# Attention and two gated feed-forward layers on one core: cosine argument rounded by a conversion to int32 on ScalarE, float64 words through a parametric ReLU

## Chip, cores, metric

One NeuronCore of one Trainium2 chip. The metric is the device time of one execution in microseconds (us), the median of several runs. Engines are called by the names of the profile: PE (TensorE), DVE (VectorE), ACT (ScalarE), POOL (GpSimd), SP (SyncE).

## What is computed

Four batches of 576 tokens, 8 heads of 64. Attention with a local mask (32 keys back) on half of the heads and a strided mask (every 32nd key) on the other half; its output, 2304 tokens by 512, runs through a layer with a cosine gate and then through a SiLU-gated layer. The weights arrive as float64.

```python
attn = softmax(mask(q @ k.T / sqrt(64)))          # per head
x = (attn @ v)                                     # 2304 x 512
h = x @ w_in                                       # 512 -> 2048
x = (h * np.cos(h)) @ w_out                        # 2048 -> 512
g, val = x @ w_gate, x @ w_val                     # 512 -> 1536 each
out = (g / (1 + np.exp(-g)) * val) @ w_out2        # 1536 -> 512
```

## The kernel before

**Stages.** One core does everything in three stages. The attention stage (until about 120 us of the span) goes through 48 groups of score tiles in a software pipeline, one step per group: matmuls for the scores (L365 to L368), maximum on DVE (L373), exponentials on ACT (L379), sums and reciprocals on DVE (L384, L388), normalisation on POOL (L389), transposes (L396, L400), copies out of PSUM on ACT (L407), the product with the values (L418) and its copy into xy (L431, L440). The first layer (until about 549 us) goes over 5 token blocks (four of 512, one of 256) and in each over 16 column tiles of w_in: such a pair is a slot. The second layer (to the end) does the same with 12 tiles of w_gate and w_val.

**Precision.** Each float32 matrix is split into a float16 high part (hi_part, L234, ACT) and a float16 low part (lo_part, L237, DVE), and every product is three float16 matmuls (mm3, L471 to L473). A slot has 12 matmuls of 512 columns for the up projection (up1), and 12 for the down projection (down1).

**Weights.** They are read as float64, 512 KB per tile of 128 by 512, as pairs of 32-bit words (load_raw, six raw buffers). conv_steps turns the words into float32: g0 multiplies the high word (read as a float32) by a power of two, on POOL in the attention stage and on ACT later; g1 takes the maximum (only for matrices that are scanned here); g2 shifts left by 3; g3 ORs in the top bits of the low word; g4 ORs in the sign of the high word and asks for the next tile. g1 to g4 are DVE instructions. w_in (16 tiles) is converted in the attention stage, w_out in the first slots of the first layer, w_gate and w_val after it, w_out2 at the end of the first layer and in the second.

**Cosine.** In slot s, up1_a turns the PSUM result ph into t = ph * turn + 1/4 (ACT, L503, into ta) and rounds t on POOL by adding and subtracting a large constant (L504), then subtracts t (L505, into tb). up1_b takes the sine on ACT (L508), one slot later; up1_c multiplies by ph on DVE (L512, which frees the PSUM bank), makes the high part on ACT (L513) and the low part on POOL (L514), two slots later. tb has three buffers, ta two, and the PSUM pool four banks.

**Order of the work.** All engines run in program order. Weight conversions lie in a list (fill) and are put between the slots by pump, which gets a budget in estimated DVE microseconds: PUMP per attention step, and in the first layer a share of the PE work of the slot. The down projections start after the first 23 up projections (HEAD = 21 plus the slots under way): until then a slot has only its 12 up matmuls and the converted g tiles are stored; after that one or two down projections come with each up projection until the stored ones are used up.

```python
later(0, hi_part ...); later(0.7, lo_part ...)      # split_chain, direct_later
budget = (work - 0.7 * n / 512) * SHARE             # work: estimated PE us of the slot
```

Of the kernel before, what the change touches and what calls it, by code (L numbers as in the profile page):

```python
# [10 lines left out]
F32 = mybir.dt.float32  # L11
F16 = mybir.dt.float16
BF16 = mybir.dt.bfloat16
I32 = mybir.dt.int32
AF = mybir.ActivationFunctionType
ALU = mybir.AluOpType
# [11 lines left out]
NBLK = len(BLOCKS)  # L28
# [11 lines left out]
MASKED = -1.0e9  # L40
MAGIC = 12582912.0
TWO_PI = 6.283185307179586
# [8 lines left out]
WARM = 11  # L51
PUMP, KP = 1.2, 5
XSAT = 9
EARLY, K0 = 1, 1
# [4 lines left out]
SHARE, SHARE2, SHARE3, SB = 0.95, 0.8, 0.4, 2  # L59
# [10 lines left out]
def build(tc, qk_l, qk_s, v_l, v_s, w_in, w_out, w_gate, w_val, w_out2, mask_l, mask_s, eye32, eye16, out):  # L70
    nc = tc.nc
    wide = w_in.dtype != F32
    with ExitStack() as ctx:
        keep = ctx.enter_context(tc.tile_pool(name="keep", bufs=1))
        ring = ctx.enter_context(tc.tile_pool(name="ring", bufs=2))
        small = ctx.enter_context(tc.tile_pool(name="small", bufs=1))
# [4 lines left out]
        quarter = small.tile([128, 1], F32, name="quarter")  # L81
        nc.vector.memset(quarter, 0.25)
        id16 = small.tile([128, 128], BF16, name="id16")
        ones16 = small.tile([128, 128], BF16, name="ones16")
# [77 lines left out]
        fill, emitted = deque(), set()  # L162
        beside_attention = True

# [21 lines left out]
        def conv_steps(mat, j, dst, scan):  # L186

            part = parts_w[mat][:, j:j + 1]
            box = {}
# [9 lines left out]
            def g0():  # L199

                t = raw[mat, j].popleft()
                box["h"], box["l"] = t[:, :, 1], t[:, :, 0]
                box["c"] = dst()
                box["u"] = box["c"].bitcast(I32)
                h = box["h"].bitcast(F32)
                if beside_attention:
                    nc.gpsimd.tensor_scalar(out=box["c"], in0=h, scalar1=2.0 ** -112, scalar2=1.0, op0=ALU.mult, op1=ALU.mult)
                else:
                    nc.scalar.activation(out=box["c"], in_=h, func=AF.Copy, scale=2.0 ** -112)

# [7 lines left out]
            def g3():  # L218
                u = box["u"]
                nc.vector.scalar_tensor_tensor(out=u, in0=box["l"], scalar=29, in1=u, op0=ALU.logical_shift_right, op1=ALU.bitwise_or)  # L220

            def g4():
                u = box["u"]
                nc.vector.scalar_tensor_tensor(out=u, in0=box["h"], scalar=-0x80000000, in1=u, op0=ALU.bitwise_and, op1=ALU.bitwise_or)  # L224
                load_raw()
            if not wide:
                return box, [(0.9 if scan else 0.35, f0)]
            return box, [(0, g0)] + [(0.63, g1)] * scan + [(0.36, g2), (0.63, g3), (0.63, g4)]

# [259 lines left out]
        acc_t, turn, c_y, half, c_o = {}, {}, {}, {}, {}  # L489
# [9 lines left out]
        def up1_a(c):  # L499
            n = c["n"]  # L500
            c["t"] = ring.tile([128, 512], F32, name="ta")[:, 0:n]
            c["w"] = ring.tile([128, 512], F32, name="tb", bufs=3)[:, 0:n]
            nc.scalar.activation(out=c["t"], in_=c["ph"], func=AF.Identity, scale=turn[c["blk"]], bias=quarter)  # L503
            nc.gpsimd.tensor_scalar(out=c["w"], in0=c["t"], scalar1=MAGIC, scalar2=MAGIC, op0=ALU.add, op1=ALU.subtract)  # L504
            nc.gpsimd.tensor_tensor(out=c["w"], in0=c["w"], in1=c["t"], op=ALU.subtract)  # L505

        def up1_b(c):
            nc.scalar.activation(out=c["w"], in_=c["w"], func=AF.Sin, scale=-TWO_PI)  # L508

# [135 lines left out]
        attn.close()  # L645
        beside_attention = False
        pacc = ctx.enter_context(tc.tile_pool(name="pacc", bufs=1, space=bass.MemoryType.PSUM))
# [80 lines left out]
        for blk in range(NBLK):  # L728
            for m in range(M1):
# [26 lines left out]
                up1_a(c)  # L756
                budget = (work - 0.7 * n / 512) * (SHARE3 if blk == NBLK - 1 else SHARE if blk < SB else SHARE2)
                pump_urgent()
# [100 lines left out]
```

## Time and profile before

| | us |
|---|---|
| median of 3 runs | 977.45 (975.25 to 980.06) |
| the profiled execution | 976.65 |
| its span, first to last instruction | 974.9 |
| busy in the span: PE, DVE, ACT, POOL | 912.2, 550.8, 393.4, 394.2 |
| mean granted clock of PE | 0.981 of full speed |

The span is cut into stretches below; in each, the engine to look at is the one whose wait ends last. Matmul durations in the trace overlap (a 512-column matmul is listed with 0.38 us and the next starts 0.215 us later), so the number of matmul records in a stretch tells how much PE work was done in it, and the busy time doesn't.

### The profile page before, as it was taken

The numbers are of one execution on the slowest core, as the hardware profiler recorded it, in microseconds if no ns is written. First come the engines' busy times: TensorE is split into PE (matmuls) and PEld (weight loads), VectorE is DVE, ScalarE is ACT, GpSimd is POOL, SyncE is SP. The second block draws the span as 40 slices with busy tenths as digits, with TensorE's granted clock in tenths as the row PEclk, the third lists the DMA queues.
The fourth block names the chain that finished last, engine by engine and source line by source line (L and its number), as shares of the span: only waits on it lengthen the run. The fifth ranks groups of instructions, "written<-read, shape, count | busy, mean of one in ns | idle before, by whom it ended". The sixth has DMA issues, their size and how long they took to land.

```text
span 974.9 us, 14438 instructions
## 1 busy us (share of the span) xinstructions
PE 912.2 (94%) x5608; PEld 473.8 (49%) x5608; DVE 550.8 (56%) x999; ACT 393.4 (40%) x829; POOL 394.2 (40%) x351
## 2 busy tenths in 40 slices
PE   7988986678799999899999999999999999999998
PEld 4666632233344444344458644444444444444587
DVE  5999776779992377895245387333323332332333
ACT  3776766554433234674346443222112221221122
POOL 3555389997557548699879400000000000000000
PEclk7999798999999999999999999999999999999999
DMA  9987741224430022207000020010001000100010
GB/s 307 348 272 200 227 167 57 65 65 126 135 108 22 22 86 88 66 1 259 1 23 22 22 65 1 1 44 1 1 1 44 0 1 1 44 1 1 1 45 22
DMA packets 21556, 72.14 MB, mean 74 GB/s; under 512 B 2704, under 2 KB 3472, under 8 KB 21488
## 3 DMA queue, kind: packets, MB, share of 16 engines
q1 hardware_dynamic: 21488, 71.22, 22.6%
q8 instruction: 44, 0.72, 0.3%
q14 instruction: 24, 0.20, 0.1%
HBM read 66.49 MB, written 4.72 MB: 73 GB/s over the span
## 4 chain that ended last, share of the span: by engine, by line
PE 66%; DVE 17%; POOL 10%; issue 4%; ACT 2%; DMA 1%; POOLq 0%; SPq 0%; ACTq 0%; DVEq 0%
PE bank L471 12%; PE bank L472 12%; PE bank L473 12%; PE acc L472 9%; PE acc L473 9%; PE acc L471 9%; POOL tb L504 5%; POOL tb L505 3%; POOL spare L514 2%; DVE spare L237 2%; DVE cv L224 1%; DVE wi L220 1%; DVE wi L224 1%; DVE ls L384 1%; DVE mx L373 1%
## 5 line engine op out<-in xcount | busy, mean ns | idle before, releaser
L471 PE MATMUL bank<-xs,spare 128*128 128x512 f16 (+1 forms) x480 | 171.7, 358 | 0.3 <-DVE ta L542 0.3
L473 PE MATMUL bank<-xs,spare 128*128 128x512 f16 (+1 forms) x480 | 171.7, 358 | 0.0
L472 PE MATMUL bank<-xs,spare 128*128 128x512 f16 (+1 forms) x480 | 171.7, 358 | 0.0
L504 POOL TENSOR_SCALAR tb<-ta 128x512 f32<-128x512 f32 (+1 forms) x80 | 148.5, 1857 | 51.1 <-ACT ta L503 45.3
L471 PE MATMUL bank<-xs,wi 128*128 128x512 f16 (+1 forms) x320 | 117.1, 366 | 38.1 <-DVE tb L512 29.5
L542 DVE SCALAR_TENSOR_TENSOR ta<-ta,bank 128x512 f32<-128x512 f32 (+1 forms) x60 | 38.0, 634 | 162.2 <-ACT ta L541 162.2
L472 PE MATMUL bank<-xs,wi 128*128 128x512 f16 (+1 forms) x320 | 117.3, 366 | 0.0
L473 PE MATMUL bank<-xs,wi 128*128 128x512 f16 (+1 forms) x320 | 117.0, 365 | 0.0
L541 ACT ACTIVATE ta<-bank,c 128x512 f32<-128x512 f32 (+1 forms) x60 | 38.6, 643 | 161.9 <-PE bank L473 161.9
L472 PEld LDWEIGHTS <-wi 128*128 128x128 f16 x560 | 55.2, 98 | 96.3 <-issue 46.1
L505 POOL TENSOR_TENSOR tb<-tb,ta 128x512 f32<-128x512 f32 (+1 forms) x80 | 97.1, 1213 | 6.7
L544 ACT ACTIVATE g<-ta 128x512 f16<-128x512 f32 (+1 forms) x60 | 35.3, 588 | 132.2 <-DVE ta L543 132.2
L472 PE MATMUL acc<-g,wi 128*128 128x512 f16 (+1 forms) x240 | 85.8, 358 | 0.2 <-DVE g L545 0.2
L471 PE MATMUL acc<-g,wi 128*128 128x512 f16 (+1 forms) x240 | 85.8, 358 | 0.0
L473 PE MATMUL acc<-g,wi 128*128 128x512 f16 (+1 forms) x240 | 85.8, 358 | 0.0
L471 PEld LDWEIGHTS <-wi 128*128 128x128 f16 x560 | 55.4, 99 | 62.2 <-issue 9.3
L473 PEld LDWEIGHTS <-wi 128*128 128x128 f16 x560 | 55.3, 99 | 56.5 <-issue 3.9
L503 ACT ACTIVATE ta<-bank,quarter,c 128x512 f32<-128x512 f32 (+1 forms) x80 | 58.0, 725 | 56.2 <-PE bank L473 52.6
L512 DVE SCALAR_TENSOR_TENSOR tb<-tb,bank 128x512 f32<-128x512 f32 (+1 forms) x80 | 50.3, 628 | 43.4 <-ACT tb L508 43.2
L472 PEld LDWEIGHTS <-spare 128*128 128x128 f16 x480 | 47.0, 98 | 46.7 <-issue 0.6
L471 PEld LDWEIGHTS <-spare 128*128 128x128 f16 x480 | 47.0, 98 | 46.4
L473 PEld LDWEIGHTS <-spare 128*128 128x128 f16 x480 | 47.0, 98 | 46.4
(127 smaller groups left out, 1602.6 us busy)
## 6 DMA issues: line engine op xcount, KB each, us to landing
raw<-w_out SPq DMA_DIRECT2D x56, 512.0 KB
raw<-w_in SPq DMA_DIRECT2D x16, 512.0 KB
raw<-w_gate SPq DMA_DIRECT2D x12, 512.0 KB
raw<-w_val SPq DMA_DIRECT2D x12, 512.0 KB
qks<-qk_s SPq DMA_DIRECT2D x8, 594.0 KB
qkl<-qk_l SPq DMA_DIRECT2D x8, 592.0 KB
out<-xy SPq DMA_DIRECT2D x16, 256.0 KB
vl<-v_l SPq DMA_DIRECT2D x8, 432.0 KB
```

Source lines behind the costliest of these rows:

```text
L224: nc.vector.scalar_tensor_tensor(out=u, in0=box["h"], scalar=-0x80000000, in1=u, op0=ALU.bitwise_and, op1=ALU.bitwise_or)
L237: nc.vector.scalar_tensor_tensor(out=dst, in0=src, scalar=s, in1=hi, op0=ALU.mult, op1=ALU.subtract)
L471: nc.tensor.matmul(out=o, lhsT=w[:, 0, c], rhs=x[0], start=first, stop=False)
L472: nc.tensor.matmul(out=o, lhsT=w[:, 0, c], rhs=x[1], start=False, stop=False)
L473: nc.tensor.matmul(out=o, lhsT=w[:, 1, c], rhs=x[0], start=False, stop=last)
L503: nc.scalar.activation(out=c["t"], in_=c["ph"], func=AF.Identity, scale=turn[c["blk"]], bias=quarter)
L504: nc.gpsimd.tensor_scalar(out=c["w"], in0=c["t"], scalar1=MAGIC, scalar2=MAGIC, op0=ALU.add, op1=ALU.subtract)
L505: nc.gpsimd.tensor_tensor(out=c["w"], in0=c["w"], in1=c["t"], op=ALU.subtract)
L512: nc.vector.scalar_tensor_tensor(out=w, in0=w, scalar=2.0 ** -14, in1=c["ph"], op0=ALU.mult, op1=ALU.mult)
L541: nc.scalar.activation(out=t, in_=pg, func=AF.Tanh, scale=half[blk])
L542: nc.vector.scalar_tensor_tensor(out=t, in0=t, scalar=1.0, in1=pg, op0=ALU.add, op1=ALU.mult)
L544: nc.scalar.activation(out=g[:, 0, 0:n], in_=t, func=AF.Copy)
```

## The change

The rounding leaves POOL. ACT now writes t = ph * turn + 1/4 as int32 into tb, by which it is rounded; up1_b forms ph * turn minus that integer on DVE (a new instruction, reading PSUM) and ACT takes sin(2 pi x + pi/2) with the bias in a one-column tile. L504 and L505 and the tile ta of the first layer are gone. In conv_steps the multiplication g0 is a parametric ReLU on ACT in all stages: with the slope 2^32 for negative inputs the exponent's bit that is moved into the sign's place by the shift is set, so g4 is gone. Budgets are reset: PUMP 1.2 to 1.0, XSAT 9 to 12 (where in the list the scale of the first token block stands), and 1.25 instead of 0.7 us of DVE taken off the budget of each slot.

```diff
-PUMP, KP = 1.2, 5
-XSAT = 9
+PUMP, KP = 1.0, 5
+XSAT = 12
...
+        right = small.tile([128, 1], F32, name="right")
+        nc.vector.memset(right, TWO_PI / 4)
...
-                if beside_attention:
-                    nc.gpsimd.tensor_scalar(out=box["c"], in0=h, scalar1=2.0 ** -112, scalar2=1.0, op0=ALU.mult, op1=ALU.mult)
-                else:
-                    nc.scalar.activation(out=box["c"], in_=h, func=AF.Copy, scale=2.0 ** -112)
+                nc.scalar.activation(out=box["c"], in_=h, func=AF.Prelu, scale=2.0 ** -112, alpha=2.0 ** 32)
...
-            def g4():
-                u = box["u"]
-                nc.vector.scalar_tensor_tensor(out=u, in0=box["h"], scalar=-0x80000000, in1=u, op0=ALU.bitwise_and, op1=ALU.bitwise_or)
                 load_raw()
...
-            return box, [(0, g0)] + [(0.63, g1)] * scan + [(0.36, g2), (0.63, g3), (0.63, g4)]
+            return box, [(0, g0)] + [(0.63, g1)] * scan + [(0.36, g2), (0.63, g3)]
...
-            c["t"] = ring.tile([128, 512], F32, name="ta")[:, 0:n]
             c["w"] = ring.tile([128, 512], F32, name="tb", bufs=3)[:, 0:n]
-            nc.scalar.activation(out=c["t"], in_=c["ph"], func=AF.Identity, scale=turn[c["blk"]], bias=quarter)
-            nc.gpsimd.tensor_scalar(out=c["w"], in0=c["t"], scalar1=MAGIC, scalar2=MAGIC, op0=ALU.add, op1=ALU.subtract)
-            nc.gpsimd.tensor_tensor(out=c["w"], in0=c["w"], in1=c["t"], op=ALU.subtract)
+            nc.scalar.activation(out=c["w"].bitcast(I32), in_=c["ph"], func=AF.Identity, scale=turn[c["blk"]], bias=quarter)
 
         def up1_b(c):
-            nc.scalar.activation(out=c["w"], in_=c["w"], func=AF.Sin, scale=-TWO_PI)
+            nc.vector.scalar_tensor_tensor(out=c["w"], in0=c["ph"], scalar=turn[c["blk"]], in1=c["w"].bitcast(I32),
+                                           op0=ALU.mult, op1=ALU.subtract)
+            nc.scalar.activation(out=c["w"], in_=c["w"], func=AF.Sin, scale=TWO_PI, bias=right)
...
-                budget = (work - 0.7 * n / 512) * (SHARE3 if blk == NBLK - 1 else SHARE if blk < SB else SHARE2)
+                budget = (work - 1.25 * n / 512) * (SHARE3 if blk == NBLK - 1 else SHARE if blk < SB else SHARE2)
```

In the changed file the lines stand at other numbers: the write as int32 is L496, the new DVE subtraction L499, the sine L501, the product with ph L505, high part L506, low part on POOL L507; g0 is L207, g1 L210, g2 L214, g3 L218, hi_part L228, lo_part L231, and L367, L378, L382 are the maximum, the sums and the reciprocals of the attention. The order of the instructions on three engines at the places that the prediction speaks of follows; names end in the number of the tile.

ACT in the head of the first layer (the slots before the first down projection), before, about one slot; a name in brackets is an engine that the instruction waits for:

```order
L508 ACTIVATE tb_2445<-tb_2445 128x512 [waits Activation_49,Pool_49]
L503 ACTIVATE ta_2504<-bank_2491,quarter_89,c6_2001 128x512 [waits PE_49,Activation_49]
L234 ACTIVATE xs_2449<-xy1_67,s10_2421 128x512
L234 ACTIVATE wo3_2143<-cv_2394,s8_2325 128x512 [waits DVE_49]
L209 ACTIVATE cv_2512<-raw_2230 128x512 [waits DMAHW1_49,Activation_49]
L513 ACTIVATE spare14_2172<-tb_2445 128x512 [waits DVE_49]
```

And in the changed kernel, two slots:

```order
L501 ACTIVATE tb_2499<-tb_2499,right_91 128x512 [waits DVE_49]
L496 ACTIVATE tb_2552<-bank_2539,quarter_89,c6_1992 128x512 [waits PE_49,Pool_49]
L506 ACTIVATE spare10_2148<-tb_2499 128x512 [waits DVE_49]
L501 ACTIVATE tb_2525<-tb_2525,right_91 128x512 [waits DVE_49]
L496 ACTIVATE tb_2578<-bank_2565,quarter_89,c12_2563 128x512 [waits DVE_49,PE_49,Pool_49]
L228 ACTIVATE wo4_2124<-cv_2506,s8_2346 128x512
L207 ACTIVATE cv_2581<-raw_2314 128x512 [waits DMAHW2_49]
L506 ACTIVATE spare9_2147<-tb_2525 128x512 [waits DVE_49]
```

The sine no longer waits for POOL but for DVE; the first instruction of a slot (L496) now waits for POOL, which must have read the tb buffer that it overwrites, the one of three slots before.

DVE at the same place, before, one slot and the start of the next:

```order
L512 SCALAR_TENSOR_TENSOR tb_2505<-tb_2505,bank_2491 128x512
L216 TENSOR_SCALAR cv_2512<-cv_2512 128x512
L237 SCALAR_TENSOR_TENSOR wo4_2144<-cv_2455,s8_2325,wo4_2144 128x512
L220 SCALAR_TENSOR_TENSOR cv_2512<-raw_2230,cv_2512 128x512
L224 SCALAR_TENSOR_TENSOR cv_2512<-raw_2230,cv_2512 128x512
L512 SCALAR_TENSOR_TENSOR tb_2534<-tb_2534,bank_2520 128x512
```

And in the changed kernel:

```order
L499 SCALAR_TENSOR_TENSOR tb_2552<-bank_2539,c6_1992,tb_2552 128x512
L218 SCALAR_TENSOR_TENSOR cv_2534<-raw_2234,cv_2534 128x512
L505 SCALAR_TENSOR_TENSOR tb_2552<-tb_2552,bank_2539 128x512
L214 TENSOR_SCALAR cv_2581<-cv_2581 128x512
L231 SCALAR_TENSOR_TENSOR wo5_2125<-cv_2534,s8_2346,wo5_2125 128x512
L499 SCALAR_TENSOR_TENSOR tb_2578<-bank_2565,c12_2563,tb_2578 128x512
```

Each slot has two instructions on the cosine instead of one, the sign's OR is gone, and fewer steps of the conversion stand in a slot.

DVE in the attention stage, before, one tile of w_in beside the steps of the attention:

```order
L212 TENSOR_REDUCE pw_in_94<-raw_497 128x1
L216 TENSOR_SCALAR wi10_81<-wi10_81 128x512
L220 SCALAR_TENSOR_TENSOR wi10_81<-raw_497,wi10_81 128x512
L388 RECIPROCAL ls_859<-ls_859 128x4
L384 TENSOR_REDUCE ls_900<-e_l1_121 128x3
L373 TENSOR_REDUCE mx_914<-bank_905 128x3
L224 SCALAR_TENSOR_TENSOR wi10_81<-raw_497,wi10_81 128x512
```

And in the changed kernel:

```order
L210 TENSOR_REDUCE pw_in_96<-raw_502 128x1
L382 RECIPROCAL ls_826<-ls_826 128x3
L378 TENSOR_REDUCE ls_861<-e_s1_119 128x4
L367 TENSOR_REDUCE mx_878<-bank_867 128x4
L214 TENSOR_SCALAR wi11_82<-wi11_82 128x512
L218 SCALAR_TENSOR_TENSOR wi11_82<-raw_502,wi11_82 128x512
```

A tile of w_in has three DVE steps instead of four; its multiplication is an ACT instruction now.

## Rows read from the trace of the kernel before

**Rows 1.** Busy time by stretch: us, engines (records), granted clock, DMA share, GB/s

```profile
20.00:92.00 72.00, 66.94 (x1088) 47.55 (x1088) 70.22 (x178) 52.35 (x210) 42.32 (x60) 0.98 0.89 285
92.00:109.00 17.00, 15.46 (x164) 10.66 (x162) 12.82 (x39) 11.73 (x40) 4.06 (x7) 0.60 0.71 214
127.00:210.00 83.00, 55.85 (x227) 23.18 (x226) 58.55 (x85) 49.07 (x80) 80.25 (x54) 0.94 0.24 78
210.00:270.00 60.00, 50.13 (x223) 22.15 (x223) 55.38 (x76) 28.30 (x47) 41.72 (x27) 0.97 0.38 114
270.00:400.00 130.00, 128.85 (x599) 58.42 (x598) 82.47 (x129) 48.58 (x81) 81.97 (x58) 1.00 0.21 67
400.00:510.00 110.00, 104.74 (x511) 49.73 (x510) 65.98 (x115) 58.11 (x100) 92.58 (x67) 1.00 0.20 70
510.00:556.00 46.00, 43.76 (x368) 35.67 (x367) 21.73 (x50) 22.77 (x52) 35.70 (x42) 1.00 0.08 24
```

**Rows 2.** POOL's groups, 127 to 210 us: busy us, mean ns, idle before

```profile
L504 POOL TENSOR_SCALAR tb<-ta 128x512 f32<-128x512 f32 x17 | 35.0, 2058 | 1.3
L505 POOL TENSOR_TENSOR tb<-tb,ta 128x512 f32<-128x512 f32 x18 | 23.9, 1328 | 1.5
L514 POOL TENSOR_TENSOR spare<-tb,spare 128x512 f16<-128x512 f32 x17 | 22.3, 1313 | 0.0
```

**Rows 3.** DVE timeline: the first L512 and the one 18 slots later

```profile
127.02 0.69 DVE L512 SCALAR_TENSOR_TENSOR tb<-tb,bank 128x512 f32<-128x512 f32 x1
...
209.84 0.69 DVE L512 SCALAR_TENSOR_TENSOR tb<-tb,bank 128x512 f32<-128x512 f32 x1 [1.24 <-ACT tb L508]
```

**Rows 4.** Waits, 127 to 210 us: total us, times, longest us

```profile
PE bank L471 <- DVE tb L512: 20.1, 10, 3.1
```

**Rows 5.** DVE's groups, 127 to 210 us

```profile
L220 DVE SCALAR_TENSOR_TENSOR cv<-raw,cv 128x512 int32<-128x512 int32 x10 | 13.8, 1381 | 0.0
L512 DVE SCALAR_TENSOR_TENSOR tb<-tb,bank 128x512 f32<-128x512 f32 x19 | 12.9, 681 | 14.7 <-ACT tb L508 14.6
L224 DVE SCALAR_TENSOR_TENSOR cv<-raw,cv 128x512 int32<-128x512 int32 x9 | 7.8, 869 | 0.1
L237 DVE SCALAR_TENSOR_TENSOR wo<-cv,s,wo 128x512 f16<-128x512 f32 x9 | 7.8, 864 | 8.9 <-ACT wo L234 8.9
```

**Rows 6.** DVE's groups, 20 to 112 us (the attention stage)

```profile
L224 DVE SCALAR_TENSOR_TENSOR wi<-raw,wi 128x512 int32<-128x512 int32 x16 | 13.2, 824 | 0.2
...
L237 DVE SCALAR_TENSOR_TENSOR wi<-wi,s,wi 128x512 f16<-128x512 f32 x6 | 4.5, 744 | 0.1
```

**Rows 7.** DVE timeline: one L220 while POOL was idle

```profile
251.69 0.69 DVE L220 SCALAR_TENSOR_TENSOR spare<-raw,spare 128x512 int32<-128x512 int32 x1
```

**Rows 8.** ACT's groups, 127 to 210 us

```profile
L503 ACT ACTIVATE ta<-bank,quarter,c 128x512 f32<-128x512 f32 x19 | 14.5, 761 | 0.0
L508 ACT ACTIVATE tb<-tb 128x512 f32<-128x512 f32 x18 | 11.3, 629 | 25.0 <-POOL tb L505 25.0
L513 ACT ACTIVATE spare<-tb 128x512 f16<-128x512 f32 x18 | 11.3, 628 | 8.1 <-DVE tb L512 7.6
...
L234 ACT ACTIVATE wo<-cv,s 128x512 f16<-128x512 f32 x9 | 6.4, 708 | 0.8 <-DVE cv L224 0.8
```

**Rows 9.** PE timeline: mask matmuls (one ends each attention step), and one stall

```profile
26.80 0.29 PE L368 MATMUL bank<-ml,id 128*128 128x288 bf16 x1
...
60.52 0.29 PE L368 MATMUL bank<-ml,id 128*128 128x288 bf16 x1
...
75.46 0.29 PE L368 MATMUL bank<-ml,id 128*128 128x288 bf16 x1
...
92.11 0.29 PE L368 MATMUL bank<-ml,id 128*128 128x288 bf16 x1
94.44 0.22 PE L123 MATMUL bank<-tops,ones 128*128 128x128 bf16 x1 [1.54 <-DVE tops L117]
```

**Rows 10.** Groups of the whole span: one of the three table loads

```profile
L508 ACT ACT_TABLE_LOAD x1 | 1.3, 1283 | 0.0
```

More of the change, by code (lines that the diff above doesn't have):

```diff
@@ L40 @@
 MASKED = -1.0e9
-MAGIC = 12582912.0
 TWO_PI = 6.283185307179586
@@ L162, in build @@
         fill, emitted = deque(), set()
-        beside_attention = True
         def later(cost, fn, key=None):
@@ L645, in build @@
         attn.close()
-        beside_attention = False
         pacc = ctx.enter_context(tc.tile_pool(name="pacc", bufs=1, space=bass.MemoryType.PSUM))
```

## The prediction

> **What bounds the kernel now.** I read the table of busy times by stretch first, because PE's own work is fixed: the change leaves every matmul in place and in its order, so time can only come out of stretches in which PE is not fed. PE work in a stretch is its matmul records times 0.215 us, the distance at which 512-column matmuls follow each other (128.85 us for 599 of them between 270 and 400) [rows 1]. From 127 to 210 us PE did 227 x 0.215 = 48.8 us of work in 83, so 34.2 us were lost; from 210 to 270, 223 x 0.215 = 47.9 of 60, 12.1 lost; from 400 to 510 it idled 5.3 and from 510 to 556 2.2 by its busy time [rows 1]. From 270 to 400, and in the second layer, there is nothing to win.
>
> What starves PE from 127 to 210 is POOL: it is busy 80.25 of 83 us [rows 1], and its three instructions of a slot take 2.06 + 1.33 + 1.31 = 4.70 us [rows 2]. The slots follow at exactly that pace: 18 of them between the two L512 shown, (209.84 - 127.02) / 18 = 4.60 us [rows 3], while a slot's 12 matmuls need 12 x 0.215 = 2.58. PE feels it as a wait for the bank that L512 frees [rows 4]. From 210 to 270 the picture is another: DVE is busy 55.38 of 60 us [rows 1]; there the conversion of w_out and w_gate sets the pace.
>
> **The head, 18 slots.** The change takes L504 and L505 off POOL, which keeps 1.31 us a slot [rows 2] and stops being the bound. What comes next? PE's floor is 2.58. For DVE I start from its 58.55 busy us [rows 1]. The nine L224 go: -7.8 [rows 5]. By the order of the instructions 18 slots of the changed kernel hold 3 ORs (L218) and 2 low parts fewer than 18 slots before, since the budget of a slot is smaller: -3 x 1.38 - 2 x 0.86 = -5.9 [rows 5]. Added are 18 subtractions L499. No row shows one; it is bounded by L512 (one PSUM, one SBUF operand, 0.681) [rows 5] and by L237 in the attention stage, which like it has a per-partition factor (0.744) [rows 6]; I take 0.744: +13.4. That makes 58.3, or 3.24 us a slot, if instructions stay as slow as they were beside a busy POOL. They don't all: L220 took 1.38 on average there and 0.69 in a moment with POOL idle [rows 5, 7], L237 0.864 against 0.744 [rows 5, 6], while L512, with one operand in PSUM, kept 0.68. Were all of it given back (7 x 0.69 + 12 x 0.12 = 6.2 us), DVE would need 52.1 us, 2.89 a slot. POOL's share falls from 97% to 1.31 / 3.05 = 43%, so I give back 57%: 54.8, 3.05 a slot. The Trainium skill ("SBUF — State Buffer", Who interferes with whom) says that a DVE instruction with two SBUF inputs and a POOL instruction that reads SBUF exclude each other for a whole instruction, and that one with a single SBUF input is not touched. The trace agrees (1.38 against 0.69 for L220, 0.68 for L512); by that rule L499, which reads PSUM, is never held up, and without it the sum would stay at 3.24.
>
> ACT: 49.07 us busy [rows 1]; the write as int32 replaces a write as float32 in the same instruction and I leave its 0.761 [rows 8]. The sine now has a bias column, which I price like L234 with its one factor column, 0.708 instead of 0.629 [rows 8]: +1.4. So 50.5 / 18 = 2.80 a slot. A new wait: L496 of a slot can't overwrite tb before POOL has read it for the low part of three slots before. That ring is high part 0.628, low part 1.31, next write 0.761 [rows 8, 2], 2.70 us, and 3.41 where one more conversion of 0.71 [rows 8] stands between write and high part on ACT, which the order shows in about a third of the slots. Queued behind a late L496 are the high part and the sine, and for these DVE waits. Four limits between 2.58 and 3.05 that hand over to each other in order: I take **3.05** and keep 2.6 and 3.4 as the ends. Gain: 18 x (4.60 - 3.05) = **27.9**; ends 34.2 (all that PE lost) and 18 x 1.2 = 21.6.
>
> **210 to 270.** DVE loses an L224 per tile and gains an L499 per slot; a slot here carries up to four tiles. At 0.869 [rows 5] against 0.744 [rows 6], some 19 ORs less and 10 subtractions more, minus the steps that the head left over (about 6, the 5.9 us above), it is near balance: -16.5 + 7.4 + 5.9 = -3.2 us, and on top of that POOL blocks less, since it is left with one instruction of 1.31 in slots of some 7 us (1 up and nearly 2 down projections, 34 x 0.215 = 7.3). PE's work then exceeds DVE's. Of the 12.1 lost I take **8** back; ends 3 and 12.
>
> **Attention.** DVE is busy 70.22 of 72 us [rows 1]; 16 L224 of 0.824 leave it, 13.2 us [rows 6]. From the mask matmul at 26.80 to that at 92.11 there are 32 steps, 2.04 us each; where PE is fed without a break (60.52 to 75.46, 8 steps) a step takes 1.87 [rows 9]. So at most 32 x 0.17 = 5.4 us are there. Against it stands that the 16 multiplications by POOL become ACT instructions; priced as the conversions that ACT already does, 0.71 [rows 8], they bring ACT from 52.35 of 72 us [rows 1] to about 63, close behind PE, and PE waits for ACT's copies in every step. I take **3**, ends 0 and 5.4. After 92 us PE stood 1.54 us for a scale from DVE [rows 9], and the granted clock between 92 and 109 was 0.60 [rows 1], mostly the lower level, 1.2 GHz. At the higher level the same 17 us would be 10.2; that 6.8 us goes into no forecast, because the changed order has the same scale in the same place.
>
> **Last slots of the first layer.** From 510 to 556 POOL's chain is shorter and PE's 2.2 us and part of the 5.3 before may close: **2**, ends 0 and 5. Nothing in the second layer: there the change only removes the sign's OR for a few tiles of w_out2, beside PE.
>
> **Sum.** 27.9 + 8 + 3 + 2 = 40.9 us off the profiled execution's 976.65: **936** (rounded). That execution is 0.8 us under the median of the runs, which the range takes in.
>
> **Rivals.**
> - *Deeper.* PE runs the head at its own pace (34), the second stretch closes but for 2 us (10), and DVE, no longer behind, has the scale ready, so that the clock doesn't fall at 92 us (6.8), with 5 in the attention steps and 3 at the end: 976.65 - 58.8 = about 918. For it: all engines' sums in the head are within 0.5 us of PE's. Against it: DVE at 3.05, and the same place of the scale.
> - *Shallower.* The tb ring and the bursts on DVE add up instead of overlapping and a head slot takes 3.6: 18.0, with 3 from the second stretch, 1 and 1 from the rest: 954. It decides once the ring's extra conversion (3.41) falls in most slots. For it: L496 waits for POOL in every slot of the order. Against: three buffers let two slots pass.
> - *ACT's write as int32 is slow.* Only at 0.761 + 1.80 = 2.56 us would ACT hold the slot at 4.60; the head then gains nothing, the rest about 5: 972, within half a percent. No row shows a write as int32 on ACT; its writes as float16 and float32 take the same 0.63 [rows 8].
> - *Slower.* The ring lets only one slot through at a time: write, subtraction, sine, product, high part, low part in series, 0.761 + 0.744 + 0.708 + 0.681 + 0.628 + 1.313 = 4.83 us. The head would lose 18 x 0.23 = 4, and of the later slots the some 30 that carry conversions would take 4.83 + 0.69 + 0.74 = 6.26 where PE has 24 x 0.215 = 5.16: 33 more, 976.65 + 37 - 3 = about 1011. It decides when a slot's chain and the conversions queued in it exceed 5.16. Against it: POOL, busy 1.31 a slot, would have to be late by two slots.
> - *Table loads.* If the parametric ReLU were in another table than exponential and sine, each of the 68 tiles would cost two loads of 1.28 us [rows 10], 174 us: 1110. The order of the changed kernel has three table loads, as many as before, so I give it 1 in 100. The Trainium skill ("ScalarE: Activation LUTs", What ACT_TABLE_LOAD costs) asks 2.66 us for every switch to another set; by that figure it would be an estimated 362 us instead of 174.
>
> **How the numbers follow.** Forecast 0.60, deeper 0.15, shallower 0.17, slow write 0.04, slower 0.03, table loads 0.01. The forecast's own range, from the ends of its terms, is about 925 to 948; down to 918 it takes in half of the deeper case, up to 954 half of the shallower one, which leaves some 2 in 10 outside. Half a percent (5 us) is about what a measurement of this kernel can tell from no change: faster 0.92, within it 0.04, slower 0.04.
>
> **What would show it.** POOL without L504 and L505 and idle for more than half of the head; 18 slots between products on DVE in about 55 us instead of 82.8; DVE the busiest engine there, at over 90%; L218 nearer 0.7 than 1.4; L499 at 0.70 to 0.75; L496 at 0.76; attention steps under 2.0 us; the second layer as long as before. I am wrong if the head's slots take over 3.4 us (then look whether L496 waits for POOL), if ACT's write or the parametric ReLU takes over 0.9 us, or if PE's clock falls in other places of the attention stage.

## The result, and the profile after

The changed kernel takes 949.6 us in the median of four runs (942.45 to 955.63); the kernel before, measured beside it, 977.6. The ratio is 0.971 [0.9633, 0.9787]. The forecast was 936, with a range from 918 to 954. The profiled execution of the changed kernel is one of the four: 946.87 us, span 944.9. By its marks the 30.0 us between the two spans (974.9 and 944.9) lie here:

| stretch | forecast | measured | marks before, after |
|---|---|---|---|
| until the first product with ph | 3 | 4.0 | 127.02, 123.00 |
| the head, 18 slots | 27.9 | 18.2 | 82.82, 64.62 |
| from there to the first store of block 0 | 8 | 8.9 | 75.41, 66.49 |
| the rest | 2 | -1.1 | 689.65, 690.79 |

The first product is the first L505 (L512 before), and the store of block 0 is its copy out of PSUM. One term is off by much, the head. The two products that bound it, in DVE's timeline of the changed kernel (start, us, instruction, idle time before and its releaser), answer to [rows 3]:

```profile
123.00 0.69 DVE L505 SCALAR_TENSOR_TENSOR tb<-tb,bank 128x512 f32<-128x512 f32 x1 [1.97 <-ACT tb L501]
...
187.62 0.69 DVE L505 SCALAR_TENSOR_TENSOR tb<-tb,bank 128x512 f32<-128x512 f32 x1 [0.89 <-ACT tb L501]
```

(187.62 - 123.00) / 18 = 3.59 us a slot, where 4.60 were before and 3.05 were forecast. Busy time by stretch in the changed kernel, with the columns of [rows 1]:

```profile
20.00:92.00 72.00, 71.41 (x1034) 50.77 (x1032) 57.83 (x168) 57.06 (x214) 26.70 (x44) 0.83 0.92 292
92.00:109.00 17.00, 17.00 (x281) 12.26 (x280) 15.87 (x44) 16.88 (x64) 6.62 (x11) 1.00 0.81 256
123.00:188.00 65.00, 51.64 (x226) 22.28 (x225) 51.80 (x88) 48.53 (x76) 21.03 (x20) 0.97 0.24 75
188.00:258.00 70.00, 67.27 (x311) 30.37 (x311) 58.20 (x104) 41.00 (x65) 13.10 (x11) 1.00 0.52 158
```

POOL, which was busy 97% of the head, is busy 32% of it now. But no other engine took its place as the bound: PE's busy time is 79% of the head, DVE's 80%, ACT's 75%. In a stage in which no engine is busy throughout, they wait for each other. The groups of that stretch (busy us, mean ns, idle before and its releasers) show that no instruction is much dearer than its price in the forecast:

```profile
L507 POOL TENSOR_TENSOR spare<-tb,spare 128x512 f16<-128x512 f32 x18 | 21.0, 1164 | 53.7 <-ACT spare L506 41.5 <-DMA raw<-w_out 12.1
L496 ACT ACTIVATE tb<-bank,quarter,c 128x512 int32<-128x512 f32 x19 | 14.6, 768 | 4.3 <-PE bank L124 2.4 <-POOL spare L507 1.9
L499 DVE SCALAR_TENSOR_TENSOR tb<-bank,c,tb 128x512 f32<-128x512 f32 x18 | 13.4, 743 | 0.0
L505 DVE SCALAR_TENSOR_TENSOR tb<-tb,bank 128x512 f32<-128x512 f32 x19 | 13.0, 685 | 5.4 <-ACT tb L501 5.2
L501 ACT ACTIVATE tb<-tb,right 128x512 f32<-128x512 f32 x18 | 12.9, 719 | 10.4 <-DVE tb L499 10.4
L231 DVE SCALAR_TENSOR_TENSOR wo<-cv,s,wo 128x512 f16<-128x512 f32 x6 | 6.5, 1075 | 4.9 <-ACT wo L228 4.9
L207 ACT ACTIVATE cv<-raw 128x512 f32<-128x512 f32 x9 | 5.8, 655 | 0.0
L218 DVE SCALAR_TENSOR_TENSOR cv<-raw,cv 128x512 int32<-128x512 int32 x7 | 5.6, 802 | 0.0
```

The subtraction takes 0.743 us (0.744 was priced), the write as int32 0.768 (0.761), the sine with a bias column 0.719 (0.708), the OR 0.802, between the 1.38 and the 0.69 of before [rows 5, 7]. The waits of the same stretch (total us, times, longest):

```profile
PE bank L465 <- DVE tb L505: 12.9, 7, 4.8
ACT tb L501 <- DVE tb L499: 10.4, 12, 1.8
DVE tb L505 <- ACT tb L501: 5.2, 12, 2.0
DVE wo L231 <- ACT wo L228: 4.9, 6, 1.6
DVE q L125 <- PE bank L124: 3.2, 1, 3.2
ACT tb L496 <- POOL spare L507: 1.9, 4, 0.7
DVE cv L214 <- ACT cv L207: 1.2, 1, 1.2
```

DVE waits 5.2 + 4.9 + 3.2 + 1.2 = 14.5 us in these rows; 1.97 of them stand ahead of the first product, which leaves 12.5 for the head. Its work, 51.80 us, makes 2.87 a slot. So DVE had less to do than the 3.05 of the forecast, and the other 0.7 us of a slot's 3.59 are waiting. They aren't spread evenly. The short slots (1 to 4, 14 and 17, counted from the first product on) take 2.73 to 2.89 us; slots 5 and 6 take 5.05 and 5.73, slot 9 4.71, slot 12 5.20, slots 15 and 16 4.01 and 4.57. The timeline of slot 12, the engines together in order of time:

```profile
162.65 0.78 ACT L496 ACTIVATE tb<-bank,quarter,c 128x512 int32<-128x512 f32 x1 [0.71 <-POOL spare L507]
163.32 0.62 ACT L506 ACTIVATE spare<-tb 128x512 f16<-128x512 f32 x1
...
163.84 0.71 ACT L228 ACTIVATE wo<-cv,s 128x512 f16<-128x512 f32 x1
...
164.02 1.16 POOL L507 TENSOR_TENSOR spare<-tb,spare 128x512 f16<-128x512 f32 x1 [1.41 <-ACT spare L506]
...
164.58 1.14 DVE L231 SCALAR_TENSOR_TENSOR wo<-cv,s,wo 128x512 f16<-128x512 f32 x1 [1.59 <-ACT wo L228]
...
165.65 0.74 DVE L499 SCALAR_TENSOR_TENSOR tb<-bank,c,tb 128x512 f32<-128x512 f32 x1
...
166.42 0.72 ACT L501 ACTIVATE tb<-tb,right 128x512 f32<-128x512 f32 x1 [1.30 <-DVE tb L499]
...
167.17 0.69 DVE L505 SCALAR_TENSOR_TENSOR tb<-tb,bank 128x512 f32<-128x512 f32 x1 [0.19 <-ACT tb L501]
...
167.91 0.38 PE L465 MATMUL bank<-xs,wi 128*128 128x512 f16 x1 [2.45 <-DVE tb L505]
```

Read it backwards. PE waits 2.45 us for the bank that L505 frees; L505 waited for the sine, the sine for the subtraction, and that stood in DVE's queue behind the low part of a converted tile, which waited 1.59 us for its high part on ACT. That stood in ACT's queue behind the slot's write and high part, and here the write itself had waited 0.71 us for POOL. Conversion and cosine cross the two engines in turn, and each hand-over is paid by both. Slots 5 and 6 follow:

```profile
134.97 0.22 PE L124 MATMUL bank<-tops,ones 128*128 128x128 bf16 x1
...
135.48 1.20 ACT L207 ACTIVATE cv<-raw 128x512 f32<-128x512 f32 x2
...
136.16 0.93 DVE L214 TENSOR_SCALAR cv<-cv 128x512 int32<-128x512 int32 x1 [1.25 <-ACT cv L207]
...
139.27 0.69 DVE L505 SCALAR_TENSOR_TENSOR tb<-tb,bank 128x512 f32<-128x512 f32 x1 [0.25 <-ACT tb L501]
...
140.01 0.58 PE L465 MATMUL bank<-xs,wi 128*128 128x512 f16 x1 [4.83 <-DVE tb L505]
...
140.39 0.63 PE L466 MATMUL bank<-xs,wi 128*128 128x512 f16 x1
...
144.15 0.22 PE L124 MATMUL bank<-tops,ones 128*128 128x128 bf16 x1
...
144.40 0.29 DVE L125 TENSOR_REDUCE q<-bank 128x1 f32<-128x128 f32 x1 [3.20 <-PE bank L124]
```

Slot 5 (134.22 to 139.27) is such a hand-over again: the shift L214 waits 1.25 us for a multiplication that stands behind write and high part on ACT, and OR, subtraction, sine and product follow one after the other. None of the three edits below that shorten the head changes this slot. Slot 6 shows something else, the scales. The small matmul of a scale (L124) takes one of PE's four banks, so the next up projection waits 4.83 us for L505. It starts at the lower level of the clock, 1.2 GHz (0.63 us listed per matmul instead of 0.38):

```profile
140.00:143.00 3.00, 2.99 (x8) 1.04 (x8) 1.17 (x5) 1.35 (x2) 1.16 (x1) 0.50 0.24 98
```

The second scale's matmul stands behind its twelve, while DVE waits for that one.

### The profile page after: what moved, and what is told of

It reads as the page before. It is cut to its first block, busy times and chain, and to the rows that moved or that the text cites. A ratio compares the mean times of both kernels' runs of the same rounds, so it can differ in the third digit from the quotient of the medians.

```text
span 944.9 us, 14190 instructions
## 1 busy us (share of the span) xinstructions
PE 909.9 (96%) x5608; PEld 474.5 (50%) x5608; DVE 505.2 (53%) x1012; ACT 410.3 (43%) x845; POOL 130.7 (14%) x175
## 3 DMA queue, kind: packets, MB, share of 16 engines
HBM read 66.49 MB, written 4.72 MB: 75 GB/s over the span
## 4 chain that ended last, share of the span: by engine, by line
PE 80%; DVE 9%; ACT 6%; issue 3%; POOL 1%; DMA 1%; SPq 0%; ACTq 0%; DVEq 0%; POOLq 0%
PE bank L465 13%; PE bank L466 13%; PE bank L467 13%; PE acc L466 10%; PE acc L467 10%; PE acc L465 10%; PE bank L359 3%; PE po L412 3%; DVE tb L505 1%; PE tp L390 1%; DVE cv L218 1%; DVE tb L499 1%; PE bank L361 1%; PE tp L394 1%; ACT wo L228 1%
## 5 line engine op out<-in xcount | busy, mean ns | idle before, releaser
L465 PE MATMUL bank<-xs,wi 128*128 128x512 f16 (+1 forms) x320 | 115.9, 362 | 19.0 <-DVE tb L505 15.3
L466 PE MATMUL bank<-xs,wi 128*128 128x512 f16 (+1 forms) x320 | 116.0, 362 | 0.0
L467 PE MATMUL bank<-xs,wi 128*128 128x512 f16 (+1 forms) x320 | 115.8, 362 | 0.0
L496 ACT ACTIVATE tb<-bank,quarter,c 128x512 int32<-128x512 f32 (+1 forms) x80 | 58.3, 729 | 70.2 <-PE bank L467 54.1
L507 POOL TENSOR_TENSOR g<-tb,g 128x512 f16<-128x512 f32 (+1 forms) x48 | 50.8, 1059 | 186.7 <-ACT g L506 163.1
L501 ACT ACTIVATE tb<-tb,right 128x512 f32<-128x512 f32 (+1 forms) x80 | 53.9, 674 | 36.7 <-DVE tb L499 36.2
L467 PE MATMUL acc<-g,wo 128*128 128x512 f16 (+1 forms) x192 | 66.0, 344 | 0.0
```

The source lines that it names most:

```text
L465: nc.tensor.matmul(out=o, lhsT=w[:, 0, c], rhs=x[0], start=first, stop=False)
L466: nc.tensor.matmul(out=o, lhsT=w[:, 0, c], rhs=x[1], start=False, stop=False)
L467: nc.tensor.matmul(out=o, lhsT=w[:, 1, c], rhs=x[0], start=False, stop=last)
L496: nc.scalar.activation(out=c["w"].bitcast(I32), in_=c["ph"], func=AF.Identity, scale=turn[c["blk"]], bias=quarter)
L507: nc.gpsimd.tensor_tensor(out=g[:, 1, 0:n], in0=w, in1=g[:, 0, 0:n], op=ALU.subtract)
```

## The experiments

The time until the first product varies from run to run with the clock in the attention stage (last section), so I compare profiles from the first product on. What lies behind it repeats well: the runs with and without fillers (below) are the same program from there on and take 821.9 and 822.3 us. The columns but the last come from one profile of each kernel. Medians are of 2 to 8 runs; each ratio is to the kernel before, timed on the same chip in the same series, so compare ratios and not medians (before took 977.6 to 981.8 in the four series). By these intervals the ReLU alone and the old budgets are faster than before, but whether by 2% is unclear; the control is the same as before.

| kernel | first product | head | a slot | first product to end | median, ratio to before |
|---|---|---|---|---|---|
| before | 127.02 | 82.82 | 4.60 | 847.9 | 977.6 |
| changed | 123.00 | 64.62 | 3.59 | 821.9 | 949.6, 0.971 [0.9633, 0.9787] |
| cosine alone | 124.23 | 64.83 | 3.60 | 829.0 | 955.4, 0.9732 [0.9669, 0.9795] |
| ReLU alone | 118.39 | 81.80 | 4.54 | 838.9 | 960.8, 0.9803 [0.9732, 0.9874] |
| early subtraction | 128.03 | 62.63 | 3.48 | 821.6 | 949.8, 0.9671 [0.9612, 0.973] |
| fillers | 120.83 | 65.06 | 3.61 | 822.3 | 947.6, 0.967 [0.9592, 0.9748] |
| four tb buffers | 123.46 | 64.07 | 3.56 | 821.3 | 945.9, 0.9652 [0.9561, 0.9743] |
| scales in their own bank | 123.46 | 61.62 | 3.42 | 818.8 | 946.7, 0.9659 [0.9564, 0.9755] |
| late low part | 123.54 | 61.31 | 3.41 | 815.1 | 937.7, 0.9568 [0.9472, 0.9665] |
| these three | 123.55 | 55.93 | 3.11 | 809.2 | 933.0, 0.9511 [0.9439, 0.9583] |
| these three, early subtraction | 127.03 | 54.19 | 3.01 | 808.8 | 934.9, 0.9542 [0.9499, 0.9585] |
| before, with two of the edits | 126.78 | 79.29 | 4.41 | 844.0 | 975.3, 0.9966 [0.9921, 1.0011] |
| changed, old budgets | 131.39 | 71.94 | 4.00 | 825.2 | 962.2, 0.9823 [0.9751, 0.9895] |

**The parts alone.** The kernel before with only the cosine's part of the change and its deduction, and with only the parametric ReLU without g4, and PUMP and XSAT; the core of the one and of the other:

```diff
-            nc.gpsimd.tensor_tensor(out=c["w"], in0=c["w"], in1=c["t"], op=ALU.subtract)
+            nc.scalar.activation(out=c["w"].bitcast(I32), in_=c["ph"], func=AF.Identity, scale=turn[c["blk"]], bias=quarter)
...
-                budget = (work - 0.7 * n / 512) * (...)
+                budget = (work - 1.25 * n / 512) * (...)
```

```diff
+                nc.scalar.activation(out=box["c"], in_=h, func=AF.Prelu, scale=2.0 ** -112, alpha=2.0 ** 32)
...
-            def g4():
```

> The cosine part alone (rounding by a write as int32, subtraction on DVE, 1.25 us off the budget of a slot), with the conversions of before (multiplication on POOL in the attention stage, OR of the sign, PUMP 1.2, XSAT 9). Theory (the head of the first layer is worth most, the conversions little): the head's slots take about 3.7 us instead of 4.60 and the attention stage ends as before, near 111 us of the span; ratio to before about 0.98. Rival (the OR of the sign is what held DVE back in the head and behind it, so the two parts only help together): slots over 4.2 us, ratio 0.99 or more.

> The parametric ReLU without the OR of the sign alone (PUMP 1.0, XSAT 12), with the cosine of before. Theory: POOL still sets 4.6 us per slot in the head, so only the attention stage and the stretch behind the head gain; ratio 0.985 to 0.995, and the time varies with how long PE stays at the lower clock in the attention stage. Rival: the attention stage at the lower clock eats all of it, ratio 1.00.

The head belongs to the cosine with its deduction: 64.83 us with them alone, 81.80 with the ReLU alone, whose slots POOL still paces. (The old budgets, below, part the two: without the smaller budgets the head of the changed kernel is 71.94.) The ReLU alone came out at 0.9803, better than the 0.985 that I had set as its best; its first product, at 118.39, is the earliest of all, and how much of that is the clock isn't settled. From the first product to the end the cosine takes 18.9 us off, the ReLU 9.0; together they take 26.0, less than the sum of 27.9 by 1.9.

**Early subtraction.** The changed kernel with the subtraction (up1_s, taken out of up1_b) ahead of the slot's conversions on DVE.

```diff
+                if steps:
+                    up1_s(steps[-1][2])
                 pump_urgent()
                 pump(budget * 0.5)
...
```

> The changed kernel with one instruction moved: the DVE subtraction of a slot is issued ahead of the conversions of the next slot, not behind them, directly before its sine. Theory (the head's 3.59 us per slot are a loop: subtraction 0.74, sine 0.72 on ACT, product 0.68, conversions, subtraction, each waiting for the one before): the loop is broken, DVE's idle time in the head falls from 13 us to under 7 and the 18 slots take 3.0 to 3.2 us, 7 to 10 us less than the changed kernel at the same clock in the attention stage. Rival (DVE's instructions are too slow beside POOL, or the tb buffers hold ACT): slots stay at 3.5 to 3.6.

The head gains 2.0 us and not the 7 to 10 that I expected, in most of the slots that were short already (2.45 to 2.67 now); the long ones stay long (4.86, 5.86, 4.50, 4.99), and the gain is gone by the end (821.6 against 821.9). So the subtraction's place behind the conversions isn't what makes the long slots long, and the loop that I expected to break isn't the main cause.

**Fillers.** Twenty-four matmuls whose result nobody reads, in the sixth attention step, to keep PE busy while the first loads arrive.

```diff
+            if k == 5:
+                t = bank()[:, 0:4 * LW].rearrange("p (n w) -> p n w", w=LW)
+                for _ in range(24):
+                    nc.tensor.matmul(out=t, lhsT=id16, rhs=ml, start=True, stop=True)
```

> The changed kernel with 24 matmuls of 384 columns, whose result nothing reads, put into one PSUM bank in step 5 of the attention, where PE waits from 11 to 15 us of the span. Theory (the changed kernel's times spread from 942 to 956 because PE is granted the lower clock from that wait on for a length that varies): no long stretch at the lower clock before 45 us, attention steps near 1.9 us from the start, time about 935, spread under 5 us. Rival (the lower clock comes from the steps themselves being too light, or the first steps wait for DMA anyway): the clock falls all the same, time 942 to 956.

The granted clock stays up until nearly 20 us, falls then all the same (0.50 from 20 to 25), and once more at 60 us. The spread of the runs remains (945.16 to 959.07). Nothing is won.

**Four tb buffers**, to test the rival that the prediction called shallower: the ring between the int32 write and POOL.

```diff
-            c["w"] = ring.tile([128, 512], F32, name="tb", bufs=3)[:, 0:n]
+            c["w"] = ring.tile([128, 512], F32, name="tb", bufs=4)[:, 0:n]
...
```

> Changed kernel with four instead of three buffers in the ring tb (room for it comes from the second layer's ta, one buffer instead of two). Ring theory (the prediction's shallower rival): the write as int32 that waits for POOL holds up sine and product; the head (18 slots from the first product on) falls from 64.6 us by 5 us or more, to under 60. Hand-over theory (the slots that are slow are slow because a low part on DVE waits for a high part on ACT, and because two scales share PE's ring of banks): the waits for POOL, 1.9 us in the whole head, go and nothing else does: head 62.7 to 64.6; from the first product to the span's end 820 to 822 us (821.9 in the changed kernel).

0.5 us in the head, 0.6 to the end: no more than two profiles of the same program differ by (the head takes 64.62 and 65.06 without and with fillers). What there is shows in slot 12, where the write had waited 0.71 us (5.20 to 4.57), and hardly elsewhere. The ring has that share and isn't the main cause.

**Scales in their own bank.** From the end of the attention stage to the end of the head (in_head) the scales use a bank that the down projections need only later.

```diff
-            t, p = bank()[:, 0:128], brief("q")
+            t, p = (pacc.tile([128, 512], F32, name="acc3") if in_head[0] else bank())[:, 0:128], brief("q")
...
```

> Changed kernel with the two scales that fall into the head computed in a PSUM bank that the down projections use later, not in PE's ring of four. Hand-over theory: PE no longer waits 4.83 us for a product before it can start the seventh up projection, DVE no longer 3.2 us for the second scale; slot 6 falls from 5.73 to about 2.7, slot 5 stays near 5 (its conversions stand in front of the product), head about 61.5 us; the short drop of the granted clock behind PE's wait (140 to 143 us) goes too. Ring theory: the two slots stay long, head 64 to 65.

Slot 6 falls from 5.73 to 2.72, slot 5 stays at 5.05; the head loses 3.0 us and the end 3.1. In PE's timeline the up projection behind the scale starts at once (this file's lines stand one further):

```profile
135.35 0.22 PE L124 MATMUL acc<-tops,ones 128*128 128x128 bf16 x1
135.42 0.38 PE L466 MATMUL bank<-xs,wi 128*128 128x512 f16 x1
...
140.67 0.22 PE L124 MATMUL acc<-tops,ones 128*128 128x128 bf16 x1 [2.50 <-DVE q L125]
```

The drop of the clock did not go, against what I expected: the second scale now waits 2.50 us from 138.17 on for the first one to be read, and matmuls behind it are listed with 0.63 us again.

**Late low part.** The low part of a tile stands behind the next tile's OR.

```diff
-                steps.insert(2, rests.popleft())
+                steps.insert(3, rests.popleft())
```

> Changed kernel in which the low part of a converted tile of w_out stands behind the OR of the next tile's low word on DVE, not ahead of it, so that its high part on ACT has one more DVE instruction's time to be made. Hand-over theory: DVE's waits for these high parts (4.9 us, six of them) fall under 2 us, slots 9, 12 and 15, 16 lose about a microsecond each; head 60 to 62 us. Load theory (a slot is long because it has more conversion work on DVE than others): the work stays, the slots only change places, head 64 to 65 us.

```profile
123.50:185.00 61.50, 52.55 (x227) 22.55 (x225) 51.77 (x88) 47.89 (x77) 21.35 (x20) 0.94 0.25 79
```

```profile
DVE wo L231 <- ACT wo L228: 0.3, 1, 0.3
```

DVE's wait for the high parts falls from 4.9 to 0.3 us, while its work stays (51.77 us against 51.80); the slots that were at 4.71, 5.20, 4.01 and 4.57 take 3.30, 4.04, 2.99 and 3.79. Slot 6 grows from 5.73 to 6.75, because the scales' wait for PE (4.2 us instead of 3.2) remains. Behind the head it wins a further 3.5 us.

**The three together**, the last three diffs in one kernel.

> The three edits together: bank of its own for the head's scales, late low parts, four tb buffers. Hand-over theory: the gains add up, 3 + 3 + 1 = 7 us, head about 57.5 us (3.2 a slot), from the first product to the end 815 us if nothing is given back later; total about 942 us. If the gain of the head is given back at the first stall behind it (as with the early subtraction), the head falls but the time from the first product to the end stays at 820 to 822 and the total at 949.

The head takes 55.93 us, 8.7 less, more than the three edits alone (3.0 + 3.3 + 0.5 = 6.8): slot 6 no longer grows (1.0 us of the difference), and slot 16 falls further, to 3.21 (0.6). Nothing is given back: 12.7 us by the end, 933.0 in the median. The busy times and the waits of its head (lines one further than in the changed kernel):

```profile
123.50:179.50 56.00, 51.08 (x227) 22.23 (x225) 51.21 (x88) 47.90 (x77) 22.17 (x20) 0.97 0.26 86
```

```profile
ACT tb L502 <- DVE tb L500: 6.5, 9, 1.8
DVE tb L506 <- ACT tb L502: 4.9, 11, 2.0
...
PE bank L466 <- DVE tb L506: 2.3, 6, 0.7
DVE cv L215 <- ACT cv L208: 1.3, 1, 1.3
```

The work is the same as in the changed kernel (DVE 51.21 against 51.80, ACT 47.90 against 48.53), done in 56 us instead of 65: DVE waits 4.9 + 1.3 = 6.2 us in these rows, 4.2 behind the first product, instead of 12.5, and is busy 91%.

**With the early subtraction as well**, its diff on top of these.

> The three edits of the best version so far and the early subtraction as well (the subtraction ahead of the slot's conversions on DVE). ACT still waits 7.8 us in the head for the subtraction there; the head falls from 55.9 by 1 to 3 us towards DVE's own 2.87 us a slot (51.7). As the early subtraction alone was given back behind the head, the time from the first product to the end stays within 2 us of 809, the total at 930 to 935. If it adds up instead: 806 or less.

1.7 us less in the head, 0.4 to the end; the totals can't be told apart. With PE at about 2.6 a slot and DVE at 2.9 there is little left in the head.

**Control.** The kernel before with the scales' bank and the late low part, which has two ORs to stand behind there.

```diff
-                steps.insert(2, rests.popleft())
+                steps.insert(4, rests.popleft())
```

> Control: the kernel before with the two edits that helped the changed kernel (scales of the head in a bank of their own, low part of a converted tile behind the ORs of the next one). Hand-over theory: they matter only where POOL is out of the way; before, POOL paces the head with 4.70 us of work a slot, so the head stays at 81.5 to 82.8 us and the total within half a percent of before (973 to 980). Rival (the two hand-overs cost before as much as after, so the edits are improvements by themselves and tell nothing on the change): head under 78 us, total 8 us or more below before.

The total can't be told from before. In the head POOL is still busy 97%:

```profile
126.80:206.10 79.30, 51.06 (x227) 21.87 (x225) 52.06 (x85) 48.40 (x80) 76.55 (x54) 1.00 0.26 82
```

```profile
L505 POOL TENSOR_SCALAR tb<-ta 128x512 f32<-128x512 f32 x17 | 33.0, 1943 | 1.3
L506 POOL TENSOR_TENSOR tb<-tb,ta 128x512 f32<-128x512 f32 x18 | 24.6, 1366 | 1.5
L515 POOL TENSOR_TENSOR spare<-tb,spare 128x512 f16<-128x512 f32 x17 | 20.0, 1178 | 0.0
```

I had expected 81.5 or more; it came to 79.3. These 3.5 us are not waiting that POOL had left uncovered: its idle time is what it was (1.3 + 1.5 us [rows 2]), and its three instructions take 4.49 us a slot instead of 4.70. DVE's OR of the low word fell as well, from 1.381 us [rows 5] to 0.864, so the likely reason is that the two engines' instructions overlap less; no run separates that. DVE's wait for the high parts of w_out, 8.9 us before [rows 5], is gone here, and the head is as long as POOL's work all the same. So POOL covered that wait before. In the changed kernel, where it doesn't, the same two edits alone are worth 3.0 and 3.3 us.

**Old budgets.** The changed kernel with PUMP 1.2 and 0.7 us taken off a slot's budget; the first block's scale stands behind tile 14.

```diff
-PUMP, KP = 1.0, 5
-XSAT = 12
+PUMP, KP = 1.2, 5
+XSAT = 14
...
-                budget = (work - 1.25 * n / 512) * (...)
+                budget = (work - 0.7 * n / 512) * (...)
```

> Changed kernel with the old budgets (1.2 per attention step, 0.7 us off a slot's budget instead of 1.25; the first block's scale stands behind tile 14, since behind tile 9 it would come before the attention has written the block). It tells what the third part of the change is worth. If the smaller budgets matter: a slot of the head carries more conversion steps, head 66 to 70 us, with less left for the stretch behind it; from the first product to the end 822 to 830. If they don't: 821 to 823. In the attention stage more DVE work per step: steps nearer 2.0 than 1.85 us, first product at 124 to 130.

```profile
131.40:203.40 72.00, 52.22 (x217) 21.86 (x217) 60.32 (x98) 54.17 (x86) 21.53 (x20) 0.95 0.35 103
```

DVE has 60.32 us of work in the head instead of 51.80, and a slot takes 4.00, more than I had expected (66 to 70 us for the head). So of the 18.2 us that the head gained, 7.3 came with less conversion work in it, and 4.0 of these are lost again behind it. The smaller budgets are part of the gain: 3.3 us by the end. The 8.4 us by which the first product comes later aren't settled by this run, because XSAT stands elsewhere than in either kernel and the clock had its drops at other times.

## Why the prediction was right, and where it was not

The bound that was to go went, and the terms other than the head came out within about 3 us of their forecasts. The measured 949.6 lies in the stated range, though not in the 925 to 948 that was given as the forecast's own; it lies in the part that the range took in from the shallower rival. (The ends of the four terms, added up, would give 920 to 952; how 925 to 948 came from them isn't said.) Of the prediction's signs POOL's idle time (68% of the head), L218, L499 and L496 came as written; DVE over 90% and 18 slots in about 55 us did not. Two of its signs of being wrong came: slots over 3.4 us, and a clock that falls in other places of the attention stage.

- **POOL's pace in the head: right.** Without L504 and L505 the slot falls below 4.60 at once, and with the cosine's part and its deduction alone as far as with the whole change (3.60).
- **DVE's sum, "54.8, 3.05 a slot": the mis-sized step, as a slot's time.** As work it was even too high: 51.80 us, 2.87 a slot. What failed is that the largest of four sums was taken for the slot ("four limits between 2.58 and 3.05 that hand over to each other in order: I take 3.05"). No term stood for waiting, and DVE waits 12.5 us in the head. The slot measured 3.59, and 64.62 - 55.93 = 8.7 of the 9.7 us that the head took beyond the forecast go with three hand-overs that three small edits take away. The evidence was in the groups of before: L237 stood 8.9 us for L234 [rows 5], and the prediction gave that wait no term. The control shows that POOL covered it as long as it was the bound; with POOL out of the way 4.9 us of such waits were left, and they counted.
- **The shallower rival: right in its size (3.6), by luck, for what was to decide it is wrong.** It put the time on the tb ring together with bursts on DVE. L496 waits 1.9 us for POOL in the whole head, and a fourth buffer wins 0.5. The long slots are those with conversions, but it is the waits among them and not their work: with the late low part DVE does the same work in 3.3 us less.
- **Contention with POOL: given back almost whole, where 57% was forecast, but not evenly.** Six of the seven ORs L218 take 0.68 or 0.69 us and one, beside an L507, 1.51. Five of the six low parts of w_out start during an L507 and take 1.14, the sixth 0.75; in the head of before eight of nine took 0.74 or 0.75. The shift L214 takes 0.41 or 0.42 us in six cases, and 0.93 and 0.88 in two that begin during an L507 (at 136.16, beside one from 135.66 to 136.82, and at 172.32). The Trainium skill ("SBUF — State Buffer", Who interferes with whom) counts a tensor_scalar in a two-port mode among what contends with POOL. The prediction had passed that clause over: its "one with a single SBUF input is not touched" holds for L499, which reads PSUM (0.743 us), and not for L214.
- **The second stretch: right**, 8.9 us for 8. PE is busy 67.27 of 70 us there.
- **Attention: right in size (4.0 for 3), partly by luck.** Two effects of some size cancel. On the one side DVE's load fell from 70.22 to 57.83 us, 32 steps at full clock take 1.88 us each (from the mask matmul at 46.59 to that at 106.64; 2.04 before), and the drop of the clock at 92 us, which the forecast had kept, is gone (1.00 in 92 to 109, 0.60 before [rows 1]). On the other a longer drop lies at the start (0.83 from 20 to 92).
- **Last slots and rest: -1.1 instead of 2.** PE stands 4.3 us for a later scale at 364 to 368, where it stood 3.0 before, and the second layer, in which nothing was to change, takes 1.7 us more (417.7 from its first high part to the end, 415.9 before). Why it does stays open.
- **Slow write, table loads, serial chain: none came.** The write takes 0.768 us, the parametric ReLU 0.655, and the trace has three table loads as before.

## What to carry to other kernels

When a change takes the bound off one engine, the next bound is not the largest sum of work but that sum plus what the engines lose in handing work to each other; look in the trace of before for waits that the old bound was covering, and price them as if uncovered. Where the busiest engine of a stage is at 80%, as here, look at the order of the queues before shortening an instruction: here two producer-consumer pairs alternate on the same two engines, and one more instruction between the halves of a pair won 3.3 us of the head; a small shared result that left the ring of the large ones won 3.0. A planner's budgets belong to the change: leaving the old ones would have cost 3.3 us of the 26 won behind the first product.

## What the runs showed of the hardware

The granted clock in the attention stage comes and goes at other places in nearly every kernel, also between programs that differ only behind it: in seven such profiles the first product comes at 123.0 to 128.0 us, and over all thirteen kernels, whose budgets differ too, at 118.4 to 131.4. At the lower level, 1.2 GHz, a step takes 3.0 to 3.4 us, at 2.4 GHz mostly 1.77 to 1.93. One of these drops, in the kernel with the scales in their own bank: PE waits for a load of values, and then runs ten microseconds at little over half the clock though it is never idle.

```profile
58.92 0.33 PE L413 MATMUL po<-pts,v_pair 118*64 118x54 f32 x4 [1.42 <-DMA v_pair<-v_s]
59.94 0.90 PE L413 MATMUL po<-pts,v_pair 118*64 118x54 f32 x12 [0.69 <-DMA v_pair<-v_s]
```

```profile
50.00:60.00 10.00, 7.89 (x130) 5.57 (x129) 8.96 (x24) 7.55 (x30) 4.49 (x8) 0.96 1.01 275
60.00:70.00 10.00, 10.00 (x105) 6.97 (x105) 3.74 (x10) 4.93 (x19) 2.51 (x4) 0.53 0.84 288
```

The four runs of the changed kernel order by it: 942.45 us at a mean clock of 0.987, 955.63 at 0.966. Why the loads of values come late in one run and not in another stays open; the DMA engines are 92% busy from 20 to 92 us of the changed kernel. The fillers didn't settle it, and loading the values earlier wasn't tried.
